# Where the small load of x stands in SP's queue, in a decode kernel that streams 81 MB

## The chip, the cores and the metric

The kernel runs on one core of a Trainium2 chip. The metric is the device time of one execution in microseconds (us). An execution has five engines that run side by side: TensorE (PE, with its weight loads shown as PEld), VectorE (DVE), ScalarE (ACT), GpSimd (POOL) and SyncE (SP). SP and ACT also issue the DMAs; their issuing shows as SPq and ACTq in the profile.

## The reference

One decode step for 8 rows. `x` is [8, 1, 512]. It is normalised, and then goes two ways: through attention over the last 2048 positions of a cache with 8 key/value heads, and through a gated feed-forward block whose output gates the attention's. All data are bf16.

```python
xn = layernorm(x)
# A: 32 query heads, 8 key/value heads of 128, window W = 2048 of 8192 positions
q = xn @ wq                                  # [8, 4096]
p = softmax(q . k_cache[:, :, -W:] * 128**-0.5)
s = (p . v_cache[:, :, -W:]) @ wo            # [8, 512]
# B: F = 1792
g = silu((sigmoid(xn @ w_gate) * (xn @ w_up)) @ w_down)
return x + s * g
```

## The kernel before

The weights and the cache's window are 81 MB, and each byte is read once. Everything large goes through one pool of 14 buffers of 1 MB, `ring`. A list `loads` holds what goes through it, in order: the two halves of `w_gate` (keys `wg`), `w_up` (`wu`) and `w_down` (`wd`), 896 KB each; the four quarters of `wq`, 1 MB each; then the 32 tiles of k and the 32 of v, 1 MB each (a tile is two key/value heads of one row of the batch), v's tile m being listed with k's tile m + 7 (`V_LAG`); and the four quarters of `wo`, the last in two pieces.

`issue_loads()` issues from this list until the ring is full: the load n needs the buffer of the load n - 14, which must have been marked by `done_with`. `load()` gives the DMAs by turns to ScalarE's queue and to SP's, ScalarE first (`queues`, `turn`). So ScalarE has the first halves of the three weights and SP the second halves; later ScalarE has nearly all v tiles and SP nearly all k tiles. The DMAs of both queues complete on a small set of eight semaphores, used in turn, so that an issue can also wait for the completion of the DMA eight issues earlier. Where an issue waits on ScalarE, what follows on ScalarE waits behind it, the activations included.

The load of x itself, 8 KB to 8 partitions (`x_bf`), doesn't go through the ring: it is a DMA of its own on SP at L79.

The order of compute is written out by hand (`manual_schedule`):

- Layer norm (L204 to L217): DVE casts x (L204) and takes its statistics (`bn_stats`, `bn_aggr`), ScalarE takes the square root of the variance (L212, after a load of its function's table), DVE inverts it (L215) and scales x to `xn_bf` (L217). PE transposes `xn_bf` (L229) and x itself (L238); the latter is kept for the last addition.
- `unit()`: gate and up projections (L253, 56 matmuls each), sigmoid (L267), down projection (L278). When the gate's matmuls are done, the two buffers of `wg` are free, and the 15th and 16th load can be issued.
- `q_projection()`: 128 matmuls (L297), then a copy of the queries to a layout with zeros (`qz_sb`, L328) on ScalarE and DVE.
- A pipeline over the 32 tiles: `k_blocks(n)` transposes the k tile on DVE (L343), `qk(n - 1)` has PE compute scores (L364), soft max for one row of the batch after every four tiles, `pv(n - 7)` has PE multiply by v (L434).
- `out_rows()` and `out_project()`: 128 matmuls with `wo` (L472), which need wo's quarters in order, then product, addition, a transpose and the store (L507 to L518).

Of the kernel before, what the change touches and what calls it, by code (L numbers as in the profile page):

```python
# [10 lines left out]
def kernel(  # L11
# [13 lines left out]
    nc = tc.nc  # L25
# [50 lines left out]


    x_bf = work.tile([B, D], bf16, name="x_bf")
    nc.sync.dma_start(out=x_bf[:], in_=A_x.flatten_outer_dims())  # L79

    queues = [nc.scalar, nc.sync]
    turn = [0]
    tiles = {}
# [6 lines left out]
    def put(key, parts):  # L90
        t = ring.tile([P, TW], bf16, name=key[0] + "_sb", tag="ring", align_bytes=ALIGN)
        tiles[key] = t
        for lo, hi, src in parts:
            load(t[:, lo:hi], src)
# [43 lines left out]
    def issue_loads():  # L138
        while issued[0] < len(loads):
            n = issued[0]  # L140
            if n >= RING and loads[n - RING][0] not in used:
                return
            put(loads[n][0], loads[n][1]())
            issued[0] += 1

    def done_with(*key):
        used[key] = True
        issue_loads()

    issue_loads()  # L150


# [4 lines left out]
    for off in range(-Hq * (NU - 1), Hq * NU, Hq):  # L157
        nc.gpsimd.affine_select(
            out=SumM[:],
            in_=SumM[:],  # L160
# [10 lines left out]
    for j in range(NU):  # L171
# [5 lines left out]
        out=off_rows[:],  # L177
        in_=off_rows[:],
# [9 lines left out]
        out=off_cols[:],  # L188
        in_=off_cols[:],
# [23 lines left out]
        out=rstd[:], in_=mv[:, 1:2], func=AF.Sqrt, bias=eps_t[:], scale=1.0  # L213
# [4 lines left out]
        out=xn_bf[:],  # L218
# [9 lines left out]
    for kt in range(KT):  # L228
        nc.tensor.transpose(  # L229
            out=xnT_ps[:, kt, :], in_=xn_bf[:B, kt::KT], identity=ident[:B, :B]  # L230
# [6 lines left out]
    for nb in range(NB):  # L237
        nc.tensor.transpose(  # L238
            out=xT_ps[:, nb, :], in_=x_bf[:B, nb * P : (nb + 1) * P], identity=ident[:B, :B]
# [246 lines left out]
    for n in range(NT + V_LAG):  # L486
# [23 lines left out]
        out=yT_sb[:].rearrange("p b nb -> p nb b"), in0=prod[:], in1=xT_sb[:], op=ALU.add  # L510
# [3 lines left out]
        out=y_ps[:], in_=yT_sb[:].rearrange("p b nb -> p (b nb)"), identity=ident[:, :]  # L514
# [4 lines left out]
        out=out.rearrange("b s (nb n) -> (b s nb) n", n=P), in_=y_sb[:]  # L519
# [31 lines left out]
```

## Time and profile before

| | |
|---|---|
| median of 3 runs | 201.81 us (201.67 to 201.96) |
| the profiled execution | 201.71 us, of which its span is 200.0 us |
| busy PE, DVE, ACT, POOL | 127.2, 114.5, 18.7, 14.2 us |
| moved by DMA | 81.29 MB, mean 406 GB/s |
| issue to landing, median: x's neighbours Wgate on ACT and SP | 4.8 and 8.1 us |
| issue to landing, median: k and v tiles | 19.5 us |
| issue of x on SP | at 0.80 us, 0.38 us long |

The page of the profile cuts the span into 40 slices of 5 us; a digit is the busy share in tenths, and GB/s is what the DMA engines moved. The chain of waits is followed back from the last instruction, each step to what released it. In the timeline a line gives start and length in us, the engine, the line of the kernel, the operation, what it writes and reads, and in brackets how long the engine was idle before it and who released it. Matmul records are pipelined, so that a busy PE is not a PE at its peak.

### The profile page before, as it was taken

Reading aid. Unit: us, or ns where it says so; the run is one execution under the profiler, and the core shown is the slowest. Engines: PE = TensorE matmul, PEld = TensorE weight load, DVE = VectorE, ACT = ScalarE, POOL = GpSimd, SP = SyncE. Lnnn points to the kernel's source line nnn. Section 1 sums busy time; section 2 is a strip of 40 time slices with the busy share of each in tenths; the row PEclk is TensorE's granted clock in tenths of the full one; section 3 lists DMA queues with packets and bytes.
Section 4 is the critical chain, followed back from the end, with each engine's and each line's share of the span. In section 5 each row is a group of like instructions: output and inputs, shape, how many; then the busy total and the mean of one; then the engine's idle time right before and its main releaser. Section 6 shows DMA issues by size and latency. Waiting matters only on the chain.

```text
span 200.0 us, 4098 instructions
## 1 busy us (share of the span) xinstructions
PE 127.2 (64%) x1793; PEld 76.3 (38%) x1793; DVE 114.5 (57%) x199; ACT 18.7 (9%) x46; POOL 14.2 (7%) x25
## 2 busy tenths in 40 slices
PE   0004948004995796996796996369644965594943
PEld 0004946001332443644353553225322633254843
DVE  2001001049998787997977997386746784717221
ACT  0003300040022002002000200110002000202000
POOL 7991000000000000000000000000000000000000
PEclk9999999999999797899888899959995899588555
DMA  6999999999999999999999999999999999999970
GB/s 205 427 425 430 429 421 424 424 428 431 426 423 429 426 426 429 419 426 423 428 421 429 428 424 428 421 429 428 423 428 428 426 419 428 426 421 424 416 299 11
DMA packets 11842, 81.29 MB, mean 406 GB/s; under 512 B 1320, under 2 KB 1328, under 8 KB 3120
## 3 DMA queue, kind: packets, MB, share of 16 engines
q10 hardware_dynamic: 6016, 41.03, 49.1%
q1 hardware_dynamic: 5808, 40.00, 47.5%
q8 instruction: 14, 0.23, 0.4%
q14 instruction: 4, 0.03, 0.0%
HBM read 81.01 MB, written 0.01 MB: 405 GB/s over the span
## 4 chain that ended last, share of the span: by engine, by line
DMA 74%; PE 11%; DVE 9%; ACT 2%; issue 1%; ACTq 1%; DVEq 0%
DMA v_sb<-in_A_v_cache_dram 48%; DMA wo_sb<-in_A_wo_dram 10%; DMA k_sb<-in_A_k_cache_dram 9%; PE s_ps L364 7%; DMA wd_sb<-in_B_w_down_dram 6%; DVE kT_sb L343 5%; PE d_ps L253 2%; DVE qz_sb L328 1%; DVE mxs L376 1%; ACTq L87 1%; ACT qz_sb L328 1%; PE a_ps L472 1%; PE o_ps L434 1%; ACT L212 1%; DVE pT_sb L407 1%
## 5 line engine op out<-in xcount | busy, mean ns | idle before, releaser
L364 PE MATMUL s_ps<-kT_sb,qz_sb 128*128 128x512 bf16 x256 | 74.9, 439 | 12.6 <-DVE kT_sb L343 12.6
L343 DVE STREAM_TRANSPOSE kT_sb<-k_sb 128x1024 uint32<-128x1024 uint32 x64 | 74.6, 1210 | 0.0
L364 PEld LDWEIGHTS <-qz_sb 128*128 128x128 bf16 x256 | 25.4, 110 | 46.8 <-issue 30.9
L434 PEld LDWEIGHTS <-v_sb 128*128 128x128 bf16 x1024 | 30.8, 99 | 6.7 <-issue 2.9
L434 PE MATMUL o_ps<-pT_sb,v_sb 128*128 128x8 bf16 x1024 | 30.3, 167 | 0.0
L393 ACT ACTIVATE p_bf<-s_ps,nm 128x512 bf16<-128x512 f32 x16 | 10.9, 683 | 112.7 <-DVE nm L389 41.3
L424 PE MATMUL den_ps<-dh,ones 128*128 128x32 f32 x16 | 4.2, 349 | 20.5 <-DVE dh L417 20.4
L407 DVE STREAM_TRANSPOSE pT_sb<-p_bf 128x512 bf16<-128x512 bf16 x16 | 10.6, 690 | 10.4 <-ACT p_bf L393 10.3
L442 DVE TENSOR_TENSOR oT_sb<-o_ps,rden 128x8 bf16<-128x8 f32 x32 | 5.3, 166 | 17.4 <-PE o_ps L434 16.9
L229 PE MATMUL xnT_ps<-ident,xn_bf 8*128 8x8 bf16 x4 | 0.3, 175 | 17.6 <-DVE xn_bf L217 17.6
L424 PEld LDWEIGHTS den_ps<-dh,ones 128*128 128x128 f32 x16 | 3.2, 249 | 21.6 <-DVE dh L417 21.5
L387 PE MATMUL mb_ps<-mj,SumM 128*128 128x4 f32 x16 | 3.1, 263 | 12.4 <-DVE mj L380 12.4
L376 DVE TENSOR_REDUCE mxs<-s_ps 128x1 f32<-128x512 f32 x16 | 10.1, 668 | 0.0
L328 DVE CAST qz_sb<-qx_ps 32x256 bf16<-32x256 f32 x8 | 3.1, 418 | 9.9 <-ACT qz_sb L328 9.9
L387 PEld LDWEIGHTS mb_ps<-mj,SumM 128*128 128x128 f32 x16 | 2.4, 188 | 15.9 <-DVE mj L380 15.9
L215 DVE RECIPROCAL rstd<-rstd 8x1 f32<-8x1 f32 x1 | 0.2, 151 | 13.0 <-ACT rstd L212 13.0
L200 POOL MEMSET qz_sb<- 128x8320 f32 x1 | 7.0, 7021 | 0.0
L229 PEld LDWEIGHTS <-xn_bf 8*128 8x128 bf16 x4 | 0.2, 115 | 17.6 <-DVE xn_bf L217 17.6
L352 PE MATMUL s_ps<-off_cols,off_rows 2*128 2x512 bf16 x16 | 6.6, 412 | 0.0
L472 PE MATMUL a_ps<-o_sb,wo_sb 128*128 128x8 bf16 x128 | 3.7, 168 | 3.1 <-DMA wo_sb<-in_A_wo_dram 1.6
L426 DVE RECIPROCAL rden<-den_ps 128x32 f32<-128x32 f32 x8 | 2.9, 358 | 4.1 <-PE den_ps L424 4.1
L297 PE MATMUL qT_ps<-xnT_sb,wq_sb 128*128 128x8 bf16 x128 | 3.7, 168 | 2.1 <-DMA wq_sb<-in_A_wq_dram 2.1
(59 smaller groups left out, 59.3 us busy)
## 6 DMA issues: line engine op xcount, KB each, us to landing
k_sb<-in_A_k_cache_dram SPq DMA_DIRECT2D x28, 1024.0 KB, 19.5
v_sb<-in_A_v_cache_dram ACTq DMA_DIRECT2D x28, 1024.0 KB, 19.5
k_sb<-in_A_k_cache_dram ACTq DMA_DIRECT2D x4, 1024.0 KB, 20.0
v_sb<-in_A_v_cache_dram SPq DMA_DIRECT2D x4, 1024.0 KB, 19.5
wq_sb<-in_A_wq_dram ACTq DMA_DIRECT2D x2, 1024.0 KB, 17.2
wq_sb<-in_A_wq_dram SPq DMA_DIRECT2D x2, 1024.0 KB, 18.7
wo_sb<-in_A_wo_dram ACTq DMA_DIRECT2D x2, 1024.0 KB, 20.5
wo_sb<-in_A_wo_dram SPq DMA_DIRECT2D x1, 1024.0 KB, 18.7
```

Of the source, the lines that this page charges most:

```text
L200: nc.gpsimd.memset(qz_sb[:].rearrange("p b w -> p (b w)").bitcast(f32), 0.0)
L328: copy(out=dst[:, :, :, c0 : c0 + HT], in_=src)
L343: nc.vector.transpose(out=kT[:], in_=tiles[("k", m)][:, cols].bitcast(u32))
L352: nc.tensor.matmul(s_tiles[(b, u)][:], lhsT=off_rows[:].rearrange("k a j r -> k (a j r)"), rhs=off_cols[:].rearrange("k a j -> k (a j)"), ...
L364: nc.tensor.matmul(s_tiles[(b, u)][:], lhsT=qz_sb[:, b, c0 : c0 + P], rhs=kv[:, x // 2, x % 2], start=False, stop=(i == NI - 1 and x == NX ...
L376: nc.vector.reduce_max(out=mxs[:, u : u + 1], in_=s_tiles[(b, u)][:], axis=AX.X)
L387: nc.tensor.matmul(mb_ps[:], lhsT=SumM[:], rhs=mj[:], start=True, stop=True)
L393: nc.scalar.activation(out=p_bf[:, u, :], in_=s_tiles.pop((b, u))[:], func=AF.Exp, bias=nm[:], scale=scale, accum_out=dens[:, u : u + 1],)
L407: nc.vector.transpose(out=pT_tiles[b][:, u * CPS : (u + 1) * CPS, :].rearrange("p c h -> p (c h)"), in_=p_bf[:, u, :],)
L424: nc.tensor.matmul(den_ps[:], lhsT=ones[:], rhs=dh[:], start=True, stop=True)
L434: nc.tensor.matmul(o_ps[:], lhsT=tiles[("v", m)][:, c * Dh : (c + 1) * Dh], rhs=pT_tiles[b][:, c, hs], start=(c == 0), stop=(c == C - 1),)
L472: nc.tensor.matmul(a_ps[:, nb, :], lhsT=w_sb[:, c0 : c0 + P], rhs=o2_sb[:, hg, j, :], start=(hg == 0 and j == 0 and nb == 0), stop=(hg == ...
```

## The change

The load of x is no longer issued ahead of the list of large loads. It is issued inside `issue_loads()`, right after the list's second entry, which is Wgate's second half and goes to SP's queue. So on SP the order of the first two DMAs is changed: Wgate's second half, then x. The DMAs of ScalarE and their order are the same.

```diff
     x_bf = work.tile([B, D], bf16, name="x_bf")
-    nc.sync.dma_start(out=x_bf[:], in_=A_x.flatten_outer_dims())
-
     queues = [nc.scalar, nc.sync]
     turn = [0]
     tiles = {}
@@ issue_loads()
             put(loads[n][0], loads[n][1]())
             issued[0] += 1
+            if n == 1:
+                nc.sync.dma_start(out=x_bf[:], in_=A_x.flatten_outer_dims())
```

## Prediction

> **What bounds the kernel now.** I read the slices of the page first, then the chain of waits, then the timeline of the first 22 us, then fine windows over the first 4 us, then the waits of ScalarE and the tile views of the loads. The slices say what the bound is:
>
> ```profile
> DVE  2001001049998787997977997386746784717221
> DMA  6999999999999999999999999999999999999970
> GB/s 205 427 425 430 429 421 424 424 428 431 426 423 429 426 426 429 419 426 423 428 421 429 428 424 428 421 429 428 423 428 428 426 419 428 426 421 424 416 299 11
> ```
>
> From the second slice to the thirty-eighth the 16 DMA engines are full and move 416 to 431 GB/s, while no compute engine is full for long. 81.29 MB at about 425 GB/s is 191.3 us. So the time is the start of the stream, 191 us of bytes, and a tail. A change that moves no byte can touch only the start, the tail, or the fullness of the stream between them. The chain of waits shows the tail:
>
> ```profile
> 174.17 20.50 DMA wo_sb<-in_A_wo_dram
> 194.66 0.05 issue
> 194.71 1.88 PE a_ps L472 x64
> 196.59 0.02 issue
> 196.61 0.20 DVE prod L507
> ```
>
> The output projection's second 64 matmuls wait for the third quarter of wo, which comes on ScalarE's queue. And the start, from the timeline:
>
> ```profile
> 0.80 0.40 ACTq L87 DMA_DIRECT2D wg_sb<-in_B_w_gate_dram  x1
> ...
> 0.80 0.38 SPq L79 DMA_DIRECT2D x_bf<-in_A_x_dram  x1
> ...
> 1.25 0.36 SPq L87 DMA_DIRECT2D wg_sb<-in_B_w_gate_dram  x1
> ...
> 2.55 0.41 DVE L204 CAST x_f<-x_bf 8x512 f32<-8x512 bf16 x1 [2.55 <-DMA x_bf<-in_A_x_dram]
> ...
> 3.83 0.06 DVE L210 MEMSET eps_t<- 8x1 f32 x1
> ...
> 10.40 4.82 ACTq L87 DMA_DIRECT2D k_sb<-in_A_k_cache_dram  x2
> ...
> 15.25 1.28 ACT L212 ACT_TABLE_LOAD   x1 [15.25 <-DMA wd_sb<-in_B_w_down_dram]
> 16.54 0.29 ACT L212 ACTIVATE rstd<-mv,eps_t 8x1 f32<-8x1 f32 x1
> ```
>
> x is here at 2.55 and its statistics are done by 3.9, but the square root waits until 15.25: ScalarE's sequencer is held in front of it by the issue of a k tile, which waits for ScalarE's half of Wdown (landed at 1.73 + 12.9 = 14.63, by the median to landing of the DMA view). So x has been ready for over 11 us when it is used.
>
> **The change part by part.** In the built order of instructions PE, DVE and GpSimd do the same in the same order; on SP the 8 KB load of x and the 896 KB load of Wgate's second half change places, and nothing else moves. The counts of bytes, packets and instructions stay.
>
> 1. *The start of the stream.* Wgate's second half is issued at 0.80 in place of 1.25, 0.45 us earlier. ScalarE issues the first half at 0.80 in both kernels, so the engines have work from the same moment on. The windows show how much the second queue could fill:
>
> ```profile
> 1.50:2.00 0.50, 0.00 (x0) 0.00 (x0) 0.00 (x0) 0.00 (x0) 0.36 (x3) 1.00 0.55 74
> 2.00:2.50 0.50, 0.00 (x0) 0.00 (x0) 0.00 (x0) 0.00 (x0) 0.43 (x2) 1.00 0.72 115
> 2.50:3.00 0.50, 0.00 (x0) 0.00 (x0) 0.41 (x1) 0.00 (x0) 0.43 (x2) 1.00 0.79 229
> ```
>
> The last two numbers are the DMA engines' busy share and GB/s. From 2.0 to 3.0 the engines are unused for 0.28 x 0.5 + 0.21 x 0.5 = 0.25 us. The bounds: a gain of the whole 0.45, if the stream really starts with SP's queue; a loss of 0.36 (the length of the issue of Wgate's half), if two large issues in the same moment have to be handed out to the engines one after the other and some of them get their first packet later. I take a gain of 0.12, half of the unused 0.25, because half of it lies ahead of any first packet. That is close to zero, and I keep both ends.
>
> 2. *x arrives later.* Behind Wgate's second half it lands between 5.6 (where the first half lands now: 0.80 + 4.8) and somewhat over 9.35 (where the second half lands now: 1.25 + 8.1). DVE's four instructions from 2.55 to 3.88 take 1.33, so the statistics are ready by 10.7 at the latest; the square root's table load starts at 15.25 or later. Cost 0; the cover is ScalarE's held sequencer, 4.5 us of it. Without that cover it would push back rstd, xn, and PE's gate matmuls (18.2) by up to 6.8 us.
>
> 3. *The two queues' order of landing.* Now ScalarE's queue runs ahead of SP's: the halves of Wgate land at 5.6 and 9.35, of Wup at 10.4 and 13.6, of Wdown at 14.6 and 18.1. With both queues starting at 0.80 with an equal load I expect them to land near their middle (7.5, 12, 16.4), so ScalarE's half of Wdown is some 1.8 us later. If SP's queue wins the start as ScalarE's does now, they change places, 3.5 us. The k issue on ScalarE, the square root, the gate matmuls (now 18.2 to 21.5) and the release of Wgate's two ring slots move with it. Who waits: the next load on ScalarE (now issued at 21.59) goes to 23.4, at most 25.1. The k loads take 13.6 us to land at the least and 19.5 at the median, in the view of k's tile, and one tile takes 4.9 us on its queue at half of 425 GB/s; so at the tightest point at least 13.6 - 4.9 = 8.7 us of work lie ahead of a load as it is issued. A shift by 1.8 or even 3.5 leaves the engines full. Cost 0; without that cover it would be the shift itself.
>
> 4. *Completion waits.* The issues from the third quarter of Wq on wait for the DMA eight issues earlier (SP's waits name Wgate, Wup and Wdown). With x in another place, that quarter on ScalarE waits for Wgate's second half instead of x (issue at 7 to 9.4 instead of about 3), the fourth on SP for Wup's first half instead of Wgate's second (10.4 to 13.6 instead of 9.33), and the first k tile on ScalarE for x instead of Wup. Behind the first waiting issue on ScalarE stand only the two k issues, then the square root, which is held to Wdown's landing anyway. Each queue still has Wdown's half and a quarter of Wq ahead. Cost 0.
>
> 5. *The tail.* If ScalarE's queue is later by 1.8 us through the whole run, the first quarter of wo (issued 169.28, 20.5 to landing: 189.8) lands at 191.6. The first 64 matmuls, 1.84 us, which start at 191.28 now, then end at 193.4, still before 194.66, when the third quarter lands. That one ends with the stream as a whole, which doesn't change. Cost 0. With 3.5 us, the first quarter lands at 193.3, the first 64 matmuls end at 195.1 and the second 64 at 197.0 in place of 196.6: a loss of 0.45.
>
> Sum, against the profiled execution: 201.71 (span 200.0 and 1.71 around it) - 0.12 + 0 + 0 + 0 + 0 = 201.59. The median of the runs shown is 201.81, 0.10 above the profiled one: **201.7 us.**
>
> A rule of the Trainium skill speaks against any worth of the change: "DMA: Bandwidth & Descriptors", section "Issuing engines are not separate DMA queues", says that DMAs of different issuing engines end on the same 16 DMA engines and interleave, so that using several issuers saves only the issuing time. The trace disagrees in part: two halves issued 0.45 us apart land 3.75 us apart, so at the start they did not share evenly. By the rule the forecast would be 201.8, by the rows it is 201.7.
>
> **The rivals.**
>
> *SP's queue wins the start (slower).* At 0.80 both sequencers issue 896 KB. Whichever reaches the engines first is served first, as ScalarE's half was by 3.75 us. For it: x, issued on SP at the same 0.80, was in at 2.55, so SP's path is not the slower one. Against: two equal loads may simply share. The place is the first wait of the output projection; it decides from the point where ScalarE's queue is more than 194.66 - 1.84 - 189.8 = 3.0 us later. Price 0.45 at 3.5 us of shift, and up to 0.36 more if the hand-out at the start is slower too: 202.2 to 202.6.
>
> *The whole 0.45 comes back (faster).* If the engines' half-empty first microseconds are for want of a second large load, the stream ends 0.45 earlier: 201.36. For it: the shares of 0.72 and 0.79. Against: a first packet's own latency can't be filled, and the unused time is only 0.25.
>
> *The early stage starves the stream (slower).* The shift of part 3 adds up with later waits until both queues run dry. Against it: 13.6 us to landing at the tightest issue. Price: up to the 3.5 us; 205.
>
> *Nothing moves.* x is not on the path and the first bytes come from ScalarE's queue: 201.8. This lies inside the forecast.
>
> **How the numbers follow.** Within 0.2% (0.4 us, about what a measurement of this kernel can tell from no change) lie the forecast and "nothing moves", and the rivals' milder forms: 0.50. Faster by more than that needs nearly the whole 0.45: 0.22. Slower: SP's queue ahead 0.23, starving 0.05, together 0.28. The range goes from 201.3, the full 0.45 below the median, to 202.5, near the end of the first rival; outside are the starving and the extreme ends. The likeliest case alone spans 201.4 to 202.1.
>
> **What would show it.** Right: DVE's cast of x waits until 7 to 9.5 and nothing but the cast, the statistics and their idle time moves with it; the table load of the square root still waits for Wdown's half, 0 to 3.5 us later; the first slice moves 205 GB/s or slightly more; slices 2 to 38 are unchanged; the chain ends over wo and the 64 matmuls. Wrong: a slice in the middle below 415 GB/s, a chain that ends over wo's first quarter, a square root that waits for DVE's statistics, or a shift of the stream's end by more than 0.4 us.

## The result, and the profile after

Seven runs of the changed kernel have a median of 202.86 us (202.23 to 203.05), seven of the kernel before beside it 202.03 us (201.67 to 202.17). The ratio is 1.0036, with an interval of 1.0022 to 1.0051: the changed kernel is slower by about 0.7 us, and the time lies above the predicted range. The profiled execution took 202.86 us, of which the span is 201.1 (before: 201.71 and 200.0).

The slices of the page, after, first:

```profile
DMA  6999999999999999999999999999999999999950
GB/s 207 422 428 429 430 420 427 424 428 427 430 419 427 430 424 430 420 427 422 430 420 428 424 425 433 420 425 427 427 428 425 425 422 427 427 425 415 417 218 5
```

The first slice moves 207 GB/s in place of 205, and no slice up to the 38th is below 415. So the stream did not start later by the page, and it did not starve. Next the timeline of the first microseconds, after:

```profile
0.80 0.41 ACTq L85 DMA_DIRECT2D wg_sb<-in_B_w_gate_dram  x1
...
0.80 0.39 SPq L85 DMA_DIRECT2D wg_sb<-in_B_w_gate_dram  x1
...
1.24 0.35 SPq L144 DMA_DIRECT2D x_bf<-in_A_x_dram  x1
...
7.98 7.85 DVE L204 CAST x_f<-x_bf 8x512 f32<-8x512 bf16 x1 [7.98 <-DMA x_bf<-in_A_x_dram]
...
8.53 7.02 POOL L200 MEMSET qz_sb<- 128x8320 f32 x1
...
15.87 0.68 DVE L206 BATCH_NORM_STATS2 stats<-x_f 8x6 f32<-8x512 f32 x1
...
17.35 1.28 ACT L212 ACT_TABLE_LOAD   x1 [17.35 <-DMA wd_sb<-in_B_w_down_dram]
18.64 0.29 ACT L212 ACTIVATE rstd<-mv,eps_t 8x1 f32<-8x1 f32 x1
```

The two halves of Wgate are issued in the same moment. x is here at 7.98 instead of 2.55, and its cast takes 7.85 us, ending just after GpSimd's memset. The square root's table load still waits for Wdown, 2.1 us later than before (17.35, was 15.25). The view of DMAs, after, has KB and the median time from issue to landing in its last columns:

```profile
wg_sb<-in_B_w_gate_dram ACTq DMA_DIRECT2D x1, 896.0 KB, 7.3
wg_sb<-in_B_w_gate_dram SPq DMA_DIRECT2D x1, 896.0 KB, 7.2
```

0.80 + 7.3 and 0.80 + 7.2: both halves land at 8.0 to 8.1. Before, they landed at 5.6 and 9.35. ScalarE's queue has lost its lead, and the loss is still there 170 us later. The timeline of the late loads, before and then after, each line a group of issues with its first start:

```profile
153.26 15.34 SPq L87 DMA_DIRECT2D v_sb<-in_A_v_cache_dram  x4
...
154.49 10.47 ACTq L87 DMA_DIRECT2D v_sb<-in_A_v_cache_dram  x3
...
164.56 0.16 DVE L389 TENSOR_REDUCE nm<-mb_ps 128x1 f32<-128x4 f32 x1 [0.48 <-PE mb_ps L387]
...
169.28 0.38 ACTq L87 DMA_DIRECT2D wo_sb<-in_A_wo_dram  x1
169.76 0.69 ACT L393 ACTIVATE p_bf<-s_ps,nm 128x512 bf16<-128x512 f32 x1 [18.07 <-DMA v_sb<-in_A_v_cache_dram]
...
172.94 0.40 SPq L87 DMA_DIRECT2D wo_sb<-in_A_wo_dram  x1
```

```profile
166.93 0.16 DVE L389 TENSOR_REDUCE nm<-mb_ps 128x1 f32<-128x4 f32 x1 [0.67 <-PE mb_ps L387]
...
171.19 0.40 SPq L85 DMA_DIRECT2D wo_sb<-in_A_wo_dram  x1
171.35 0.39 ACTq L85 DMA_DIRECT2D wo_sb<-in_A_wo_dram  x1
171.84 0.69 ACT L393 ACTIVATE p_bf<-s_ps,nm 128x512 bf16<-128x512 f32 x1 [18.26 <-DMA v_sb<-in_A_v_cache_dram]
```

Before, ScalarE issues its first quarter of wo 3.66 us ahead of SP; after, the two issue within 0.16 us, ScalarE 2.07 later and SP 1.75 earlier than before. And right behind ScalarE's issue stands the exponential of the soft max of the 7th row of the batch (L393). Its input, the maximum `nm`, is ready at 164.72 before and 167.09 after, 4.8 to 5.0 us ahead of its use. The exponential starts when the issue in front of it is through, and so it is late by 2.08 us, as the issue is. The tail of the timeline, before and then after:

```profile
191.28 1.84 PE L472 MATMUL a_ps<-o_sb,wo_sb 128*128 128x8 bf16 x64 [1.51 <-DVE o_sb L461]
194.71 1.87 PE L472 MATMUL a_ps<-o_sb,wo_sb 128*128 128x8 bf16 x64 [1.58 <-DMA wo_sb<-in_A_wo_dram]
```

```profile
193.62 2.65 PE L472 MATMUL a_ps<-o_sb,wo_sb 128*128 128x8 bf16 x94 [1.50 <-DVE o_sb L461]
196.63 1.07 PE L472 MATMUL a_ps<-o_sb,wo_sb 128*128 128x8 bf16 x34 [0.37 <-issue]
```

The wait of 1.58 us for wo is gone: the output projection starts 2.34 us later, and by then wo is there. 2.34 - 1.58 = 0.76, and 0.37 of idle time that the profile gives no releaser for, make the 1.12 us by which the matmuls end later (197.70, was 196.58). The chain of waits, after, shows the way there:

```profile
151.50 19.79 DMA v_sb<-in_A_v_cache_dram
171.29 0.03 ACTq L85
...
171.84 0.79 ACT p_bf L393 x2
172.66 1.38 DVE pT_sb L407 x2
...
192.20 1.28 DVE o_sb L461
193.62 2.65 PE a_ps L472 x94
```

Before, this chain ended over a transfer of wo; now a transfer of v releases ScalarE's issue, the issue the exponential, and from there it is compute to the end. In this execution wo itself isn't late: its third quarter lands at 176.24 + 18.3 = 194.5 (before: 194.66).

### The profile page after: what moved, and what is told of

It reads as the page before. It is cut to its first block, busy times and chain, and to the rows that moved or that the text cites. A ratio compares the mean times of both kernels' runs of the same rounds, so it can differ in the third digit from the quotient of the medians.

```text
span 201.1 us, 4098 instructions
## 1 busy us (share of the span) xinstructions
PE 129.1 (64%) x1793; PEld 76.9 (38%) x1793; DVE 122.0 (61%) x199; ACT 18.7 (9%) x46; POOL 14.1 (7%) x25
## 4 chain that ended last, share of the span: by engine, by line
DMA 65%; PE 14%; DVE 13%; ACT 2%; issue 2%; ACTq 1%; DVEq 0%
DMA v_sb<-in_A_v_cache_dram 48%; DMA k_sb<-in_A_k_cache_dram 9%; DMA wd_sb<-in_B_w_down_dram 7%; PE s_ps L364 6%; DVE kT_sb L343 6%; PE o_ps L434 3%; DVE pT_sb L407 2%; PE a_ps L472 2%; PE d_ps L253 2%; DVE qz_sb L328 1%; DVE mxs L376 1%; ACTq L85 1%; ACT qz_sb L328 1%; PE den_ps L424 1%; ACT p_bf L393 1%
## 5 line engine op out<-in xcount | busy, mean ns | idle before, releaser
L364 PE MATMUL s_ps<-kT_sb,qz_sb 128*128 128x512 bf16 x256 | 76.7, 447 | 14.2 <-DVE kT_sb L343 14.2
L393 ACT ACTIVATE p_bf<-s_ps,nm 128x512 bf16<-128x512 f32 x16 | 10.9, 683 | 113.2 <-DMA v_sb<-in_A_v_cache_dram 71.5
L407 DVE STREAM_TRANSPOSE pT_sb<-p_bf 128x512 bf16<-128x512 bf16 x16 | 10.7, 696 | 9.4 <-ACT p_bf L393 9.3
L442 DVE TENSOR_TENSOR oT_sb<-o_ps,rden 128x8 bf16<-128x8 f32 x32 | 5.3, 165 | 18.3 <-PE o_ps L434 17.7
L204 DVE CAST x_f<-x_bf 8x512 f32<-8x512 bf16 x1 | 7.9, 7853 | 8.0 <-DMA x_bf<-in_A_x_dram 8.0
## 6 DMA issues: line engine op xcount, KB each, us to landing
wo_sb<-in_A_wo_dram ACTq DMA_DIRECT2D x2, 1024.0 KB, 18.3
```

Source lines behind the costliest of these rows:

```text
L204: nc.vector.tensor_copy(out=x_f[:], in_=x_bf[:])
L364: nc.tensor.matmul(s_tiles[(b, u)][:], lhsT=qz_sb[:, b, c0 : c0 + P], rhs=kv[:, x // 2, x % 2], start=False, stop=(i == NI - 1 and x == NX ...
L393: nc.scalar.activation(out=p_bf[:, u, :], in_=s_tiles.pop((b, u))[:], func=AF.Exp, bias=nm[:], scale=scale, accum_out=dens[:, u : u + 1],)
L407: nc.vector.transpose(out=pT_tiles[b][:, u * CPS : (u + 1) * CPS, :].rearrange("p c h -> p (c h)"), in_=p_bf[:, u, :],)
```

## The experiments

The theories, as the expectations call them. A: ScalarE's queue has lost its lead, its issues come about 2 us later through the whole run, and the exponentials behind them push the end of compute past the end of the stream. B: the late square root and gate matmuls move everything after them. C: the start or the end of the stream itself is later. All ratios are against the kernel before, run on the same chip.

**The lead given back.** The changed kernel with one more 8 KB load, of a tile that nobody reads, first on SP. x stays behind Wgate's half.

```diff
+    x_pad = work.tile([B, D], bf16, name="x_pad")
+    nc.sync.dma_start(out=x_pad[:], in_=A_x.flatten_outer_dims())
```

> The changed kernel with one more 8 KB load of x, to a tile that nobody reads, ahead of Wgate's half on SP; x itself stays behind Wgate. So SP's first large load is late again by one small one, and x is late as in the changed kernel. Theory A (ScalarE's queue lost its lead over SP's, its loads land 2 us later for the whole run, and the exponentials that stand behind its issues come 2 us later, so that compute ends after the stream): the lead is back, Wgate's halves land about 3.7 us apart, the seventh row's exponential is at about 170, time 202.0 (201.8 to 202.2). Theory B (x late: DVE's cast of x takes 7.9 us beside GpSimd's memset, the statistics are ready at 16.8 only, and the early stage's lateness runs through to the end): cast long, square root later than before by 1.5 us or more, 202.6 to 202.9.

Measured: 201.91 us, ratio 0.9998 (0.9989 to 1.0006). Its timeline:

```profile
9.59 6.25 DVE L206 CAST x_f<-x_bf 8x512 f32<-8x512 bf16 x1 [9.59 <-DMA x_bf<-in_A_x_dram]
...
169.62 0.69 ACT L395 ACTIVATE p_bf<-s_ps,nm 128x512 bf16<-128x512 f32 x1 [18.06 <-DMA v_sb<-in_A_v_cache_dram]
```

x comes even later than in the changed kernel, the exponential is back at 169.62, and the time is back. So where x stands costs nothing; what costs is that both queues begin with a large load at once. The waits for older completions aren't it either: ScalarE's second quarter of wq is issued at 9.35 here, even later than in the changed kernel (7.99). The square root ran only 0.26 us later than before, so this run says little on B.

**The square root late.** The kernel before, with two more activations ahead of the square root, whose result is not read.

```diff
+    late = work.tile([P, 1024], f32, name="late")
+    nc.vector.memset(late[:], 0.0)
+    for _ in range(2):
+        nc.scalar.activation(out=late[:], in_=late[:], func=AF.Sqrt)
```

> The kernel before with two more square roots over 128x1024 elements on ScalarE, whose result nobody reads, ahead of the square root of the variance: the early stage starts about 2 us later, while the loads and their order are those of before and ScalarE's queue keeps its lead. Theory A: the seventh row's exponential at about 169.8 as before, time 202.0 (201.8 to 202.2). Theory B: 202.8.

Measured: 201.93 us, ratio 0.9998 (0.9990 to 1.0007). Its timeline:

```profile
18.71 0.28 ACT L216 ACTIVATE rstd<-mv,eps_t 8x1 f32<-8x1 f32 x1
...
170.03 0.69 ACT L397 ACTIVATE p_bf<-s_ps,nm 128x512 bf16<-128x512 f32 x1 [17.93 <-DMA v_sb<-in_A_v_cache_dram]
```

The square root starts at 18.71, later than in the changed kernel (18.64), and it costs nothing. B falls.

**The zeros by VectorE.** The changed kernel, with the memset of `qz_sb` on DVE instead of GpSimd.

```diff
-    nc.gpsimd.memset(qz_sb[:].rearrange("p b w -> p (b w)").bitcast(f32), 0.0)
+    nc.vector.memset(qz_sb[:].rearrange("p b w -> p (b w)").bitcast(f32), 0.0)
```

> The changed kernel with the zeros of qz_sb (128x8320 words) written by DVE ahead of its cast of x instead of by GpSimd. If GpSimd's memset beside it is what stretches the cast of x from 0.41 to 7.85 us, the cast takes 0.41 again. Theory A: ScalarE's square root waits for Wdown's half in any case, time as of the changed kernel, 202.8. Theory B: better by what the statistics come earlier, at most 0.6.

Measured: 202.61 us, ratio 1.0038 (1.0023 to 1.0053). Its timeline:

```profile
2.61 6.99 DVE L200 MEMSET qz_sb<- 128x8320 f32 x1 [2.61 <-issue]
9.52 0.35 DVE L204 CAST x_f<-x_bf 8x512 f32<-8x512 bf16 x1
```

The stretched cast of the changed kernel is GpSimd's memset beside it; without it the cast takes 0.35 us. The time stays up, so the cast isn't the cause. In this execution the end waits for the stream again: wo's third quarter lands at 195.63, and the second 64 matmuls wait 0.96 us for it.

**x on GpSimd's queue.** The kernel before with this edit; SP then starts with Wgate's half as in the changed kernel.

```diff
-    nc.sync.dma_start(out=x_bf[:], in_=A_x.flatten_outer_dims())
+    nc.gpsimd.dma_start(out=x_bf[:], in_=A_x.flatten_outer_dims())
```

> The kernel before with the load of x issued by GpSimd's queue at its very start: x is early, and both other queues begin with their half of Wgate at the same moment, as in the changed kernel. Theory A: the lead is lost as in the changed kernel, Wgate's halves land within 0.5 us of each other, the seventh row's exponential at about 171.8, time 202.7 to 202.9. Theory B: the statistics are early, no long cast, time 202.0.

Measured: 202.80 us, ratio 1.0049 (1.0037 to 1.0062), as A says. But the run was meant to have x early, and its view of DMAs has

```profile
x_bf<-in_A_x_dram POOLq DMA_DIRECT2D x1, 8.0 KB, 6.2
```

x took 6.2 us behind the two halves of Wgate, and so the run doesn't tell A from B, which the late square root did.

**x first on ScalarE's queue.** The kernel before, so that SP would lead instead.

```diff
-    nc.sync.dma_start(out=x_bf[:], in_=A_x.flatten_outer_dims())
+    nc.scalar.dma_start(out=x_bf[:], in_=A_x.flatten_outer_dims())
```

> The kernel before with its first load of x on ScalarE's queue instead of SP's, so that Wgate's second half starts on SP ahead of the first half on ScalarE. Theory A: SP's queue leads now; ScalarE's loads land some 3.5 us later than in the kernel before, the seventh row's exponential at about 173.3 instead of 169.8, time 203.4 to 204.5. Theory B: x lands at 2.6 as before, statistics early, time 202.0.

Measured: 202.08 us, ratio 1.0003 (0.9994 to 1.0012): a miss. SP did lead at first (Wgate in at 6.0 on SP and 10.8 on ScalarE). Then SP's issues waited for compute that had become later, in its view of waits from 40 to 85 us:

```profile
SPq L87 <- DVE kT_sb L343: 21.4, 4, 11.7
...
SPq L87 <- PE o_ps L434: 11.9, 2, 10.0
```

The columns are the sum, the number and the longest of the waits. Before, in the same stretch, the sums are 6.7 and 8.7, the longest 2.0 and 6.1. Later ScalarE's queue leads again (first quarter of wo issued at 168.60, SP's at 174.78), and the exponential starts at 169.09. This agrees with A at its last step (no late exponential, no loss), and shows what I had left out: a lead isn't fixed at the start, waits for ring buffers can shift it.

**wo on SP.** The changed kernel with all pieces of wo on SP, so that no issue stands in front of the 7th row's exponential.

```diff
-    def load(dst, src):
-        queues[turn[0] % 2].dma_start(out=dst, in_=src)
+    def load(dst, src, on_sync=False):
+        q = nc.sync if on_sync else queues[turn[0] % 2]
+        q.dma_start(out=dst, in_=src)
...
-            load(t[:, lo:hi], src)
+            load(t[:, lo:hi], src, on_sync=key[0] == "wo")
```

> The changed kernel with all loads of wo on SP's queue. So no issue of wo stands ahead of the last rows' exponentials on ScalarE; the start, x included, is that of the changed kernel. Theory A: the seventh row's exponential starts when its maximum is ready, at about 167.1 instead of 171.8, the output projection's matmuls can begin before 191, and the end is the stream's again: 201.7 (201.4 to 202.1). Theory B: the early stage is as late as in the changed kernel, time 202.8.

Measured: 202.40 us, ratio 1.0018 (1.0009 to 1.0026). Its timeline:

```profile
167.42 0.69 ACT L394 ACTIVATE p_bf<-s_ps,nm 128x512 bf16<-128x512 f32 x1 [13.82 <-DVE nm L390]
...
196.75 0.59 PE L473 MATMUL a_ps<-o_sb,wo_sb 128*128 128x8 bf16 x16 [0.64 <-DMA wo_sb<-in_A_wo_dram]
```

The exponential now starts 0.3 us after its maximum, and about half of the loss is gone. The rest is a new wait, for wo's last piece at 196.70. That wo now comes on one queue may have part in it, but the other profiles with both queues starting at once and wo on both have it at 196.24 to 196.78 as well, all but the first of the changed kernel (195.75).

**The exponential ahead of the issue.** In the changed kernel, issues are held back while the soft max of a row is between its two phases, and then made up.

```diff
+    hold = [False]
...
-        issue_loads()
+        if not hold[0]:
+            issue_loads()
...
+            hold[0] = False
+            issue_loads()
...
+        if soft and ph == 0:
+            hold[0] = True
```

> The changed kernel with the loads that fall due between the maximum and the exponential of a row of the batch held back until that row's exponential is issued, so that on ScalarE the exponential stands ahead of the issue that waits for an older transfer. Queues, order of the loads and the start are those of the changed kernel. Theory A (what costs the time is the exponential behind the issue): the seventh row's exponential starts right after its maximum, at about 167.2 instead of 171.8; the output projection's first matmul at about 191 instead of 193.6; wo's last pieces land as in the changed kernel, at 194.5 and 195.8; time 201.7 to 202.0. Theory B (the early stage's 2 us of lateness): that is unchanged, 202.8.

Measured: 202.32 us, ratio 1.0016 (1.0007 to 1.0025). Its timeline:

```profile
162.97 0.16 DVE L391 TENSOR_REDUCE nm<-mb_ps 128x1 f32<-128x4 f32 x1 [0.56 <-PE mb_ps L389]
...
167.72 0.69 ACT L395 ACTIVATE p_bf<-s_ps,nm 128x512 bf16<-128x512 f32 x1 [18.12 <-DMA v_sb<-in_A_v_cache_dram]
...
195.22 1.87 PE L474 MATMUL a_ps<-o_sb,wo_sb 128*128 128x8 bf16 x64 [1.71 <-DMA wo_sb<-in_A_wo_dram]
```

The exponential is 4.1 us earlier, compute waits for wo again, and the chain ends over the transfer as before the change. It does not start right after its maximum, as I had expected: that came earlier by 4 us too, and the exponential now stands behind the issue before, of a tile of v at 167.08. Over half of the loss is gone, yet not all: the third quarter of wo is here at 195.2, where the kernel before has it at 194.66. That is C, a second cost.

**The same in the kernel before.**

> The kernel before with the same holding back as in the changed kernel with the exponential first. Theory A2 (two costs: the exponential held behind the issue, and a stream that ends up to half a microsecond later because both queues hand out their first large load at once): the start is the staggered one of before, so the stream ends as in before, wo's third quarter lands at 194.6 to 194.9; time 201.9 to 202.1. If the holding back itself costs the 0.3 us that were left in the changed kernel with the exponential first: 202.3.

Measured: 201.84 us, ratio 0.9990 (0.9981 to 0.9999). Its timeline:

```profile
165.06 0.69 ACT L395 ACTIVATE p_bf<-s_ps,nm 128x512 bf16<-128x512 f32 x1 [18.23 <-DMA k_sb<-in_A_k_cache_dram]
...
194.59 1.87 PE L474 MATMUL a_ps<-o_sb,wo_sb 128*128 128x8 bf16 x64 [1.82 <-DMA wo_sb<-in_A_wo_dram]
```

This is the fastest version, if by little. In both kernels with the exponential first, the end waits for wo's third quarter, and so their difference is that of the stream: 0.63 us in the profiles (195.22 and 194.59), 0.26% or 0.5 us in the ratios.

**wo's third quarter in two pieces**, on top of the exponential first in the changed kernel.

```diff
-        cuts = ((0, 2),) if h < 3 else ((0, 1), (1, 2))
+        cuts = ((0, 2),) if h < 2 else ((0, 1), (1, 2))
```

> As the one with the exponential first, and the third quarter of wo also cut into two pieces, one on each queue, so that less work is left after the last landing. Theory A: 0.2 to 0.3 less than the one without the cut, 201.5 to 201.8; Theory B: 202.8.

Measured: 202.65 us, ratio 1.0038 (1.0025 to 1.0051): a miss. The last piece lands at 196.40, as it does without the cut (196.41), so the smaller pieces end no sooner. Why the time is above that of the uncut version I can't say; its profiled span, 200.5, is the same, but that execution, 202.23 us, was the fastest of the seven.

**The changed kernel again**, as it is, in a later set of runs.

> The changed kernel as it is, beside the other runs of this chip, and a second profile of it: 202.7 to 202.9; the profile's last landing of wo shows how far the stream's end scatters from 195.75 (Theory A2: up to 196.7, as in the other kernels with both queues starting at once).

Measured: 203.10 us, ratio 1.0055 (1.0042 to 1.0067). Its timeline:

```profile
172.69 0.69 ACT L393 ACTIVATE p_bf<-s_ps,nm 128x512 bf16<-128x512 f32 x1 [17.95 <-DMA v_sb<-in_A_v_cache_dram]
...
194.07 3.56 PE L472 MATMUL a_ps<-o_sb,wo_sb 128*128 128x8 bf16 x128 [1.49 <-DVE o_sb L461]
```

The same picture, a little later: 194.07 - 191.28 - 1.58 = 1.2 us by the profile, 1.1 by the ratio. Here wo is later too: the third quarter lands at 195.41 (194.5 in the first profile of this kernel), the last piece at 196.64 (195.75). So in this execution the stream alone would have made the end 0.75 us later, and compute only adds the rest.

**The lead taken and given by cutting wq.** In the kernel before, the first two quarters of wq are cut so that ScalarE has 11/16 of each; in the changed kernel so that SP has it.

```diff
-        return [(0, TW, A_wq.rearrange("(p kt) n -> p kt n", kt=KT)[:, kt, :])]
+        v = A_wq.rearrange("(p kt) n -> p kt n", kt=KT)[:, kt, :]
+        cuts = ((0, 2816), (2816, TW)) if kt < 2 else ((0, TW),)
+        return [(lo, hi, v[:, lo:hi]) for lo, hi in cuts]
```

(In the changed kernel 1280 in place of 2816.)

> The kernel before, whose start is staggered, with the first two quarters of wq cut in two pieces of 11/16 (ScalarE's queue) and 5/16 (SP's), 0.79 MB more for ScalarE's queue in all, so that its later loads land some 1.8 us later and its lead is gone from then on. Theory A2: the first cost alone: the seventh row's exponential at about 171.5 instead of 169.8, the output projection begins at about 193, the stream ends as in before; time 202.4 to 202.7. If only the start counts: 202.0.

> The changed kernel with the same two quarters cut the other way, 5/16 for ScalarE's queue and 11/16 for SP's: both queues start at once, but ScalarE's is ahead from 25 us on as in the kernel before. Theory A2: the second cost alone: exponential at about 170, the output projection's first part not late, wo's third quarter at 194.7 to 195.3; time 202.1 to 202.4. If the lead is all that counts: 202.0; if only the start counts: 202.8.

Measured: 202.15 us, ratio 1.0002 (0.9994 to 1.0011), and 202.74 us, ratio 1.0041 (1.0028 to 1.0054). Both missed, since the edit did not move the lead: the exponential stays at 170.26 in the one and 171.70 in the other. With rows of 5.6 KB on one queue and 2.5 KB on the other, the larger pieces took no longer than the smaller ones, so that the longer rows got the larger share of the engines. The runs leave the lead untested, and show once more that the time goes with the order of the first issues. The chain of the second, though, ends otherwise than the changed kernel's:

```profile
176.01 19.56 DMA wo_sb<-in_A_wo_dram
195.57 0.05 issue
195.62 1.88 PE a_ps L474 x64
```

Its output projection starts at 192.75, 1.47 us later than in the kernel before, and still waits 1.02 us for wo's third quarter, which is 0.91 us late. So the whole loss of this execution is the stream's, as in the one with the zeros by VectorE. Compute and stream both end later when the two queues start at once, and the later of them sets the time: the two costs are not added up.

What the runs settle is in this table, the ratio of each to the kernel before (the cells are from different sets of runs, each against its own runs of the kernel before):

| | SP starts with a small load | both start with a large load |
|---|---|---|
| exponential behind the issue | 1 (the kernel before) | 1.0036, again 1.0055 (the changed kernel) |
| exponential ahead of the issue | 0.9990 | 1.0016 |

Down the right column, 0.2 to 0.4%, 0.4 to 0.8 us, is what the exponential's place is worth once ScalarE's queue has lost its lead; the interval of the 1.0036 still overlaps that of the 1.0016, that of the 1.0055 doesn't. Down the left it is 0.1%, at the edge of what the runs can tell, for there compute had 1.58 us to spare. Across the lower row, 0.26%, is what the stream pays at its end for the start in the same moment.

## Why the prediction was wrong

**The bound and the start (parts 1 and 3).** Right: stream and tail set the time, the halves share evenly, the square root waits for Wdown's half and comes about 2 us later (1.8 predicted, 2.1 measured), the stream starves nowhere. The windows of the first microseconds, after, columns as in part 1:

```profile
1.50:2.00 0.50, 0.00 (x0) 0.00 (x0) 0.00 (x0) 0.00 (x0) 0.36 (x3) 1.00 1.44 172
2.00:2.50 0.50, 0.00 (x0) 0.00 (x0) 0.00 (x0) 0.00 (x0) 0.43 (x2) 1.00 0.46 86
2.50:3.00 0.50, 0.00 (x0) 0.00 (x0) 0.00 (x0) 0.00 (x0) 0.41 (x2) 1.00 0.60 201
```

Before, they were 0.55 and 74, 0.72 and 115, 0.79 and 229. (A packet counts in the window in which it starts, so a share can be above 1.) Up to 5.0 us the windows sum to 1.04 MB after and 1.03 before: in this execution the start is neither fuller nor emptier. The seven other profiles with both large loads handed out at once have 0.95 to 0.99 MB by then, the six with the loads apart 0.99 to 1.08, a loss of some 0.1 us at 425 GB/s in place of the gain of 0.12. The end of the stream shows more of it. wo's third quarter lands at 194.55 to 194.92 in the six with the loads apart; with the loads at once, and wo loaded as in the changed kernel, it lands at 194.5 in the first profile and at 195.0 to 195.6 in five others. So part 1 has the wrong sign, with the first profile an exception; I had this case as the bound of +0.36, and the two kernels with the exponential first give some 0.5 for the stream's end. How the one makes the other is only argued: some engines may get their first packets late and, if each of them has a fixed share of every transfer, end late.

**x late (part 2).** Cost 0 was right, as the added load on SP shows, but the cover was mis-sized. I had the statistics ready by 10.7 and 4.5 us to spare. The cast, 0.41 us in the row I used, fell beside GpSimd's memset and took 7.85, and DVE's four instructions ended at 16.8, 0.6 us ahead of the table load.

**Completion waits (part 4).** Right: ScalarE's quarter of wq is held for Wgate's second half, SP's for Wup's first, and nothing comes of it.

**The tail (part 5): the step that failed.** I moved the landing of wo's first quarter by 1.8 us and left the matmuls' start at 191.28, as if that were a property of compute. But the same 1.8 us moves ScalarE's issues, and an exponential stands behind one of them. The start became 193.62 by the chain exponential, p's transposes, matmuls with v, `o_sb`. Compute had 1.58 us to spare, which I could read from the row of the second 64 matmuls and did not weigh against the shift. Set against it, a shift of 2.1 gives 2.1 - 1.58 = 0.5 at this term in place of 0; it measured 0.76 and the 0.37 without a releaser. That is the profiled execution, with the stream on time; where the stream was late as well (by 0.75 us in the second profile), the wrong sign of part 1 had a share in the miss, and in two other kernels that start both queues at once the stream alone set the end.

**The rivals.** "SP's queue wins the start" had nearly the right price, 202.2 to 202.6, and the right side, but not the mechanism: SP wins nothing (8.1 and 8.0), and the place is not the wait for wo's first quarter. Its side remark, a slower hand-out at the start, is the part that the runs support. "The whole 0.45 comes back" is refuted by the sum of the windows and the landings of wo, starving by the slices.

**The rule.** "DMA: Bandwidth & Descriptors", section "Issuing engines are not separate DMA queues", says that DMAs of all issuers share the same engines and that several issuers save only issuing time. Sharing is what the changed kernel shows, 8.1 and 8.0. But in the kernel before, a start 0.45 us apart gives landings 3.75 us apart and a lead that is there at 169 us; losing it cost 0.36% and 0.55% here, the joint start included.

**Open.** Why a joint hand-out leaves the end of the stream late in most executions and not in all, and why the changed kernel's runs scatter (202.23 to 203.05 in the first set) more than those before. A kernel in which ScalarE's queue loses its lead with the first hand-outs still apart was tried twice by cutting wq and not reached, so the two costs were separated at the exponential, not at the lead.

## What to carry to other kernels

When a queue of transfers is issued by an engine that also computes, ask of every shift in its transfers which instruction of that engine stands behind the next issue, and carry the shift through it to the end; a start of compute read from the trace is not a constant. Where the end waits for two things, the later one sets it: mending one of them gains only what the other leaves. Before a shift is priced at nothing, set it against the slack of the late stage, here one wait of 1.58 us in the chain. And of two queues with equal loads, the order of the first issue can set which of them leads for the whole run: a load that seems to be in the way may be what sets them apart.

## What the runs showed of the hardware

- Two loads of 896 KB issued 0.45 us apart on two queues landed 3.75 us apart, and issued together 0.1 us apart. In the kernel before, an offset of a few microseconds between the queues was still there at 169 us (3.66 us); it isn't bound to last, for with x first on ScalarE's queue the lead that SP began with was lost again.
- A cast of 8x512 elements took 7.85 us beside a GpSimd memset of 7.02 us, and 0.35 us with that memset on VectorE. "SBUF — State Buffer", section "SBUF: two separate sides", says that the two engines share a pair of ports, which one instruction locks for its whole length, VectorE's in some of its modes only; whichever starts first gets it. The trace agrees on the blocking. By its starts the cast (7.98) was ahead of the memset (8.53) and yet ended after it, but an earlier instruction of GpSimd (6.27 to 8.58) was still running when the cast began.
- A load of 8 KB issued by GpSimd took 6.2 us behind two loads of 896 KB; on SP ahead of them it was here at 2.55.
- With rows of 5.6 and 2.5 KB, the longer ones got the larger share of the engines: pieces of 704 KB took 13.7 us to land at the median, pieces of 320 KB on the other queue 14.5 (10.9 and 15.6 with the queues exchanged).
